# Gate weights written one loop step earlier, and the turning of keys and queries spread over two steps, in an attention and expert kernel

## The chip, the cores and the metric

The kernel runs as one program on 1 core of a Trainium2 chip. The metric is the device time of one execution in microseconds (us), lower is better. The kernel before took 427.58 us (median of 3 runs, 426.6 to 427.71).

## The reference

Two computations follow each other. First, attention in chunks: 4 batches of 8 heads, 768 tokens, 64 channels. A chunk of 32 queries sees 8 memory keys and at most 56 keys around the chunk.

```python
for c in range(nc):                                   # 24 chunks of 32 queries
    k_full = np.concatenate([mem_k, k_ctx], axis=2)
    v_full = np.concatenate([mem_v, v_ctx], axis=2)
    scores = scale * np.matmul(q_c, k_full.transpose(0, 1, 3, 2))
    scores = scores - np.max(scores, axis=-1, keepdims=True)
    a = np.exp(scores)
    a = a / (np.sum(a, axis=-1, keepdims=True) + 1e-09)
    out[:, :, c_start:c_end] = np.matmul(a, v_full)
```

Its result, 3072 tokens of 512 channels, goes through a layer of 8 experts. Each token goes to the one expert with the largest logit:

```python
logits = x @ w_gate + modality_bias[modality_id]
e_idx = np.argmax(logits, axis=1)
for e in range(E):
    mask = e_idx == e
    h = np.maximum(x[mask] @ w1[e], 0.0)
    out[mask] = gate_w[mask, None] * (h @ w2[e])
```

## The kernel before, in words

The 32 heads are taken in 16 pairs, u = 0 to 15. The main loop has two steps for each pair, i = 2u for the first half of its queries (hf 0) and i = 2u + 1 for the second (hf 1), and two more at the end, 34 in all. The text counts steps and pairs from 0, as the code does, so "the ninth step" is step 8, and the sixth pair is pair 5. All five instruction streams run in the order in which the program is written; nothing reorders them.

The work is a pipeline. In step i TensorE (PE) computes the scores of half i (`scores`, L328), turns the exponents' input of half i - 1 (`trans_p`, L345), turns keys or queries of the next pair, turns the attention output of half i - 2 (`trans_x`, L382) and multiplies half i - 1 with the values (`attend`, L357). VectorE (DVE) subtracts the row maximum (`less_max`, L336 and L339) and divides by the row sum (`normalize`, L365 to L370). ScalarE (ACT) takes the exponent (L347) and copies what PE has turned from PSUM to SBUF.

The part that the change touches prepares pair u + 1 while pair u is computed. Before it, step 2u turned the keys of both heads (`trans_k`, L310 and L314), which ACT copied into the block-diagonal key tile `kbd` in four copies (`store_k`, L320); DVE regrouped the queries (`regroup_q`, L277) into the single buffer `qr`. Step 2u + 1 then turned both halves of the queries (`trans_q`, L292), which ACT copied to `qT` (`store_q`, L297). `kbd` has two buffers, a pair's own being u % 2. What PE turns goes through four PSUM banks taken in rotation (`bank`).

GpSimd (POOL) copies the rows that neighbouring chunks share within the value tile `vw` (`share`, L267), writes the memory keys (`mem_keys`, L302), and issues the stores of the attention output to DRAM (`store_x`, L375). SyncE (SP) issues all loads of q, k and v in order: at the end of step 2u the values of pair u + 2 (`load_v`, L254 to L256), the memory values (`load_mv`, L263) and the keys and queries of pair u + 4 (`load_qk`, L93).

After each four pairs (one batch) the routing of its tokens starts, a generator `route(b)` of which `pump` issues a few instructions at a time between those of the steps. Its first matmuls (L530) read the gate weights `wg3`, which `gate_weights` (L233 to L235) writes on POOL; the bias rows come from `bias_rows` behind it. Their small loads are issued in step 5 (L170 to L173). Later the routing builds one-hot tables on POOL (the first two tiles) and DVE (the others), L656 and L659, which PE multiplies (L667) before it goes on. After the loop come the experts, up to L1300, with weights that SP loads by the routing's result.

```python
        if i == 9:
            gate_weights()
            bias_rows()
```

Of the kernel before, what the change touches and what calls it, by code (L numbers as in the profile page):

```python
# [37 lines left out]
NPOOL = 2  # L38
NSPIN = 8
NVW = 3  # L40
ORDERED = {mybir.EngineType.PE, mybir.EngineType.SP, mybir.EngineType.Pool, mybir.EngineType.Activation, mybir.EngineType.DVE}


@with_exitstack
def tile_chunk_attention_top1_moe(
# [14 lines left out]
    nc = tc.nc  # L60
    scale = 1.0 / float(D) ** 0.5
    NU = B * H // 2

    ctx.enter_context(tc.manual_schedule(engines=ORDERED))
    const = ctx.enter_context(tc.tile_pool(name="const", bufs=1))
# [17 lines left out]
    def bank():  # L83
        return ps.tile([P, 512], F32, name="tr", tag="tr", bufs=4)

    q2s, k2s = {}, {}
# [25 lines left out]
    kbds = [(pers if i else rt).tile([P, NCH, 2, 64], F32, name=f"kbd{i}") for i in range(2)]  # L112
    vws = [(rt if i == 1 else pers).tile([P, 2, NCH, D + 1], F32, name=f"vw{i}") for i in range(NVW)]
    zero = const.tile([P, 1], F32, name="zero")
# [14 lines left out]
    def blank_v(i, parts=1):  # L129
        for h in range(2):  # L130
            for k in range(parts):
                c = slice(NCH * k // parts, NCH * (k + 1) // parts)
                nc.gpsimd.memset(vws[i][64 * (1 - h):64 * (2 - h), h, c].rearrange("p c d -> p (c d)"), 0.0)
# [99 lines left out]
    def gate_weights():  # L233
        nc.gpsimd.memset(wg3, 0.0)
        nc.gpsimd.tensor_copy(wg3.rearrange("p c (q x) -> p c q x", x=40)[:, :, :, 0:E], wg.unsqueeze(2).to_broadcast([P, 4, 3, E]))  # L235
# [9 lines left out]
    qrs, qTs, xTs, xbs, PTs, kts, qts, scs, sbs, avs = ({} for _ in range(10))  # L245

    def load_v(u):
        vw = vws[u % NVW]
        for h in range(2):
            hh = 2 * u + h  # L250
            r0 = 64 * h

            src = bass.AP(tensor=vf.tensor, offset=(hh * S + 8) * D, ap=[[D, 32], [32 * D, NCH - 1], [1, D]])
            nc.sync.dma_start(vw[r0 + 24:r0 + 56, h, 0:NCH - 1, 0:D], src)  # L254
            nc.sync.dma_start(vw[r0 + 24:r0 + 48, h, NCH - 1, 0:D], vf[hh * S + S - 24:hh * S + S])
            nc.sync.dma_start(vw[r0 + 16:r0 + 24, h, 0, 0:D], vf[hh * S:hh * S + 8])  # L256

    def load_mv(u):
        vw = vws[u % NVW]
        for h in range(2):  # L260
            hh = 2 * u + h
            r0 = 64 * h
            nc.sync.dma_start(vw[r0 + 56:r0 + 64, h].rearrange("p c d -> p (c d)"), mvx[hh // 16][8 * (hh % 16):8 * (hh % 16) + 8].rearrange("p c d -> p (c d)"))  # L263

    def share(u, h, copy):
        vw, r0 = vws[u % NVW], 64 * h
        copy(vw[r0:r0 + 24, h, 1:NCH, 0:D], vw[r0 + 32:r0 + 56, h, 0:NCH - 1, 0:D])  # L267

    def share_v(u):
        for h in range(2):  # L270
            share(u, h, nc.gpsimd.tensor_copy)

    def regroup_q(u):
        q2 = q2s.pop(u)
        qr = qrs[u] = wk.tile([P, 6, 2, D], F32, name="qr", bufs=1)
        eng = nc.gpsimd if u in (1, 2) else nc.vector
        eng.tensor_copy(  # L277
            qr.rearrange("p x h d -> p h x d"), q2.rearrange("p (h a) (j d) -> p h (a j) d", h=2, j=2)
        )

    def warm(t, k):
        for _ in range(k):
            nc.tensor.matmul(t, idle[:, 0:P], idle[:, P:640], start=True, stop=True)

    def trans_q(u):
        qr = qrs.pop(u)
        for j in range(2):
            t = qts[u, j] = bank()
            if u == 1 and j == 0:
                warm(t, 5)  # L290
            for i in range(3):
                nc.tensor.transpose(t[:, i:3 * P:3], qr[:, 2 * i + j].rearrange("p h d -> p (h d)"), ident)  # L292

    def store_q(u, j):
        if j == 0:
            qTs[u] = wk.tile([P, S], F32, name="qT")
        nc.scalar.copy(qTs[u].rearrange("p (s j) -> p s j", j=2)[:, :, j], qts.pop((u, j))[:, 0:384])  # L297

    def mem_keys(u, eng):
        for h in range(2):  # L300
            r = slice(64 * h, 64 * h + 64)
            eng.tensor_copy(kbds[u % 2][r, :, h, 56:64], memT[r, u:u + 1, :].to_broadcast([64, NCH, NMEM]))  # L302

    def trans_k(u):
        k2 = k2s.pop(u)
        for h in (1, 0):
            hh = 2 * u + h
            t = kts[u, h] = bank()
            for i in range(3):
                nc.tensor.transpose(t[:, 9 + i:9 + i + 3 * P:3], k2[:, 3 * h + i, :], ident)  # L310

            pads = bass.AP(tensor=t.tensor, offset=t.offset + 1, ap=[list(t.ap[0]), [392, 2], [1, 8]])
            mem_sel = ident[:, 4 * hh:4 * hh + 4].unsqueeze(1).unsqueeze(1)
            nc.tensor.matmul(pads, mkp, mem_sel.to_broadcast([P, 2, 2, 4]), start=True, stop=True)  # L314

    def store_k(u, h, j, copy):
        tt = kts[u, h][64 * j:64 * j + 64]
        win = bass.AP(tensor=tt.tensor, offset=tt.offset + 1, ap=[list(tt.ap[0]), [16, NCH], [1, 28]])
        dst = kbds[u % 2][64 * h:64 * h + 64, :, h, 0:56]
        copy(dst.rearrange("p c (i j) -> p c i j", j=2)[:, :, :, j], win)  # L320
# [30 lines left out]
    def attend(u, hf):  # L351
        vw, PT = vws[u % NVW], PTs.pop((u, hf))
        avb = avs[u, hf] = ps.tile([P, 512], F32, name="av", tag="av", bufs=2)
        for t in range(3):
            for j in range(4):
                c = 4 * (3 * hf + t) + j
                nc.tensor.matmul(  # L357
                    avb[32 * j:32 * j + 32, t * W:(t + 1) * W], PT[:, t * P + 32 * j:t * P + 32 * j + 32],
                    vw[:, :, c, :], start=True, stop=True,
                )  # L360
# [32 lines left out]
    def pump(k, pe=(), late=False):  # L393
        if now[0] >= 2 * NU - 6 and not late:
            return
        while k > 0 and routing:
            g, wait, b, since = routing[0]
            if wait:
                if wait not in pe or since == now[0] and b < B - 2:
                    return  # L400
                pe = ()
            r = next(g, None)
            if r is None:
                routing.pop(0)
                return
            routing[0] = (g, r if r != "v" else None, b, now[0])
            k -= r == "v"
# [524 lines left out]
    def first_keys(u, copy):  # L932
        for h in range(2):
            r = slice(64 * h, 64 * h + 64)
            copy(kbds[u][r, :, h, 56:64], memp[r, u * NMEM:(u + 1) * NMEM].unsqueeze(1).to_broadcast([64, NCH, NMEM]))

    first_keys(0, nc.vector.tensor_copy)
    trans_q(0)
    store_q(0, 0)
    store_q(0, 1)  # L940
# [13 lines left out]
    n = len(units)  # L954
    for i in range(n + 2):
        live = i < n
        u, hf = units[i] if live else (NU, i % 2)
# [9 lines left out]
        if live:  # L967
# [11 lines left out]
                nc.vector.tensor_copy(memT.rearrange("p u m -> p (u m)"), memp[:, 0:P])  # L979
                load_mv(2)  # L980
            pump(1)
        if u + 1 < NU and hf == 0:
            if 0 < u < NU - 2:
                mem_keys(u + 1, nc.gpsimd)
            trans_k(u + 1)
            if 0 < u < NU - 2:
                regroup_q(u + 1)
            if u == 1:
                blank_v(2)
            pump(1)  # L990
            store_k(u + 1, 1, 0, nc.scalar.copy)
            if u == 0:
                first_keys(1, nc.scalar.copy)
            store_k(u + 1, 1, 1, nc.scalar.copy if u > 3 else nc.vector.tensor_copy)
            if u > 0:
                store_k(u + 1, 0, 0, nc.scalar.copy)
            store_k(u + 1, 0, 1, nc.scalar.copy if u > 0 else nc.vector.tensor_copy)
            pump(1)
        elif u + 1 < NU:
            if u == 0:  # L1000
                store_k(1, 0, 0, nc.scalar.copy)
            if u == NU - 2:
                share(u + 1, 0, nc.gpsimd.tensor_copy)
            else:
                share_v(u + 1)
            trans_q(u + 1)
            store_q(u + 1, 0)
            store_q(u + 1, 1)
            pump(3)
        elif live:  # L1010
            pump(3)
# [42 lines left out]
                routing.append((route(u2 // 4), "tiled", u2 // 4, i))  # L1054
        for _ in range(4 if i > 2 and hf == 1 else 0):
            next(constants, None)
        if i == 9:
            gate_weights()
            bias_rows()
        if i == 5:  # L1060
            nc.scalar.copy(mvx[1][:, :, 0:D], mvn[:, 1:2].to_broadcast([P, NCH, D]))
        if i == n - 5:
            regroup_q(NU - 1)
        if i < n:
            pump(1, ("tiled",))
        if i < 2:
# [1 line left out]
        if live and hf == 0 and u >= 1:  # L1068
            if u - 1 + NVW < NU:
                load_v(u - 1 + NVW)  # L1070
# [256 lines left out]
```

## Time and profile before

| | us |
|---|---|
| median of 3 runs | 427.58 |
| the profiled execution's own time | 428.59 |
| its span, first to last instruction | 426.8 |
| PE busy | 407.6 (95%) |
| DVE busy | 334.1 (78%) |
| ACT busy | 298.6 (70%) |
| POOL busy | 238.6 (56%) |

The span is the time from the first to the last instruction of the profiled execution; its own time is longer by what lies around the span. Busy times are sums over instructions of an engine. A wait is idle time of an engine ahead of an instruction, put down to what released it.

### The profile page before, as it was taken

The page shows a single profiled execution, that of the slowest core. Times are in us where ns is not written, and L with a number is a line of the kernel's source. Part 1 is how long each engine was busy: PE and PEld are TensorE (multiplying, and loading weights), DVE is VectorE, ACT ScalarE, POOL GpSimd, SP SyncE. Part 2 cuts the span into 40 slices and gives each one's busy share as a digit, 9 for nine tenths or more (in the row PEclk, how much of TensorE's full clock was granted, in tenths as well). Part 3 has the DMA queues.
Part 4 walks back from the last instruction along what each step waited for, and adds up shares of the span by engine and source line. Part 5 has one row for each costly group of instructions (what it writes and reads, how often), then busy time and mean ns, then how long its engine had stood idle before and what let it go on. Part 6 is the DMA issues. An engine that isn't in the chain of part 4 may idle for free.

```text
span 426.8 us, 11396 instructions
## 1 busy us (share of the span) xinstructions
PE 407.6 (95%) x3872; PEld 342.6 (80%) x3875; DVE 334.1 (78%) x788; ACT 298.6 (70%) x594; POOL 238.6 (56%) x320
## 2 busy tenths in 40 slices
PE   8899699999899999999999999999999999999993
PEld 5678478888776888989898887888888788888882
DVE  6989468879687878958979889768789787988750
ACT  7677667868685556746657677868878676888750
POOL 8886567668583445767754574354666266520101
PEclk9999999999999999999999999999999999999998
DMA  9899899999957920125423729979776514320101
GB/s 221 146 261 228 193 235 210 223 239 192 232 156 201 271 52 1 55 77 121 99 78 72 272 64 266 290 231 297 231 282 196 157 54 102 73 77 2 50 3 55
DMA packets 82543, 66.81 MB, mean 157 GB/s; under 512 B 50659, under 2 KB 71339, under 8 KB 82476
## 3 DMA queue, kind: packets, MB, share of 16 engines
q1 hardware_dynamic: 75276, 46.36, 45.0%
q0 software_dynamic: 6784, 19.50, 15.0%
q8 instruction: 33, 0.54, 0.5%
q14 instruction: 34, 0.28, 0.2%
q10 hardware_dynamic: 416, 0.13, 0.1%
HBM read 84.64 MB, written 12.76 MB: 228 GB/s over the span
## 4 chain that ended last, share of the span: by engine, by line
PE 71%; issue 12%; ACT 6%; POOL 4%; DVE 4%; DMA 2%; POOLq 0%; ACTq 0%
PE av L842 12%; PE tr L830 11%; PE sc L842 10%; PE tr L811 9%; PE av L357 5%; PE tr L814 5%; ACT kbd L320 4%; PE sc L328 4%; PE tr L382 3%; PE tr L345 2%; PE tr L292 2%; PE tr L310 2%; PE tr L530 2%; DMA out_dram<-o,ix_now 1%; POOL xg L751 1%
## 5 line engine op out<-in xcount | busy, mean ns | idle before, releaser
L811 PE MATMUL tr<-xt,w 128*128 128x512 f32 x256 | 70.1, 395 | 0.0
L742 DVE TENSOR_TENSOR w<-raw,w 128x512 fp32r<-128x512 f32 x96 | 64.7, 719 | 4.0 <-ACT w L741 3.2
L842 PE MATMUL av<-wh,h 128*128 128x512 f32 x192 | 61.5, 393 | 0.0
L267 POOL COPY vw<-vw 24x1472 f32<-24x1472 f32 x31 | 44.2, 1425 | 21.8 <-DMA vw<-in_v_dram 20.6
L741 ACT CAST w<-raw 128x512 fp32r<-128x512 f32 x96 | 53.9, 623 | 1.5 <-DMA raw<-in_moe_w_dram 1.5
L842 PE MATMUL sc<-wh,h 128*128 128x512 f32 x160 | 50.8, 392 | 0.0
L811 PEld LDWEIGHTS tr<-xt,w 128*128 128x128 f32 x256 | 44.3, 189 | 7.2 <-issue 0.8
L830 PE MATMUL tr<-xt,w 128*128 128x256 f32 x384 | 48.1, 284 | 0.7 <-DVE xt L806 0.7
L830 PEld LDWEIGHTS tr<-xt,w 128*128 128x128 f32 x384 | 46.8, 191 | 2.0 <-DVE xt L806 1.0
L320 ACT COPY kbd<-tr 64x672 f32<-64x672 f32 x57 | 44.5, 781 | 4.3 <-DVE kbd L320 2.3
L814 PEld LDWEIGHTS tr<-xt,w 128*128 128x128 f32 x256 | 39.2, 189 | 5.4
L847 POOL DMA_INDIRECT out_dram<-o,ix_now x22 | 26.1, 1184 | 29.6 <-ACT o L846 24.3
L842 PEld LDWEIGHTS av<-wh,h 128*128 128x128 f32 x192 | 36.0, 188 | 7.5 <-issue 0.2
L814 PE MATMUL tr<-xt,w 128*128 128x256 f32 x256 | 40.7, 281 | 0.0
L820 DVE TENSOR_TENSOR hs<-tr,hs 128x256 f32<-128x256 f32 x64 | 26.8, 419 | 17.6 <-ACT hs L817 17.6
L842 PE MATMUL av<-wl,h 128*128 128x512 f32 x96 | 37.5, 390 | 0.0
L821 ACT ACTIVATE h<-hs 128x256 fp32r<-128x256 f32 x64 | 26.8, 419 | 14.8 <-DVE hs L820 13.7
L751 POOL DMA_INDIRECT xg<-gd,gx x24 | 27.1, 1128 | 14.7 <-DMA gd<-gt 9.0
L842 PEld LDWEIGHTS sc<-wh,h 128*128 128x128 f32 x160 | 30.0, 188 | 6.3 <-issue 0.2
L823 DVE TENSOR_TENSOR wl<-vw,wh 128x512 fp32r<-128x512 f32 x48 | 33.2, 691 | 2.2
L824 DVE SCALAR_TENSOR_TENSOR h<-hs,h 128x256 fp32r<-128x256 f32 x64 | 27.7, 433 | 7.7 <-ACT h L821 7.3
L776 POOL COPY planes<-xg 128x1024 uint16<-128x1024 uint16 x18 | 24.0, 1339 | 17.0 <-DMA xg<-xd,gx 16.9
(266 smaller groups left out, 910.4 us busy)
## 6 DMA issues: line engine op xcount, KB each, us to landing
raw<-in_moe_w_dram SPq DMA_DIRECT2D x96, 256.0 KB
vw<-in_moe_w_dram SPq DMA_DIRECT2D x72, 256.0 KB
k<-in_k_dram SPq DMA_DIRECT2D x16, 384.0 KB
q<-in_q_dram SPq DMA_DIRECT2D x16, 384.0 KB
xd<-xb POOLq DMA_DIRECT2D x16, 384.0 KB
kbd<-in_moe_w_dram SPq DMA_DIRECT2D x24, 256.0 KB
vw<-in_v_dram SPq DMA_DIRECT2D x32, 184.0 KB
xall<-in_moe_w_dram SPq DMA_DIRECT2D x4, 1024.0 KB
```

The costliest lines, as they stand in the source:

```text
L267: copy(vw[r0:r0 + 24, h, 1:NCH, 0:D], vw[r0 + 32:r0 + 56, h, 0:NCH - 1, 0:D])
L320: copy(dst.rearrange("p c (i j) -> p c i j", j=2)[:, :, :, j], win)
L741: nc.scalar.copy(wh[i], raw[i])
L742: (eng or nc.vector).tensor_sub(wl[i], raw[i], wh[i].bitcast(F32))
L751: nc.gpsimd.indirect_dma_start(out=xg[t][:, part], out_offset=None, in_=rows, in_offset=bass.IndirectOffsetOnAxis(ap=gx[:, t:t + 1], axis=0))
L811: nc.tensor.matmul(ph, wh[f][:, c * P:(c + 1) * P], xt[:, c].rearrange("p a n -> p (a n)"), start=(c == 0), stop=False, skip_group_check=True)
L814: nc.tensor.matmul(ph[:, 0:256], wl[f][:, c * P:(c + 1) * P], xth[:, c], start=False, stop=(c == 3), skip_group_check=True)
L820: nc.vector.tensor_add(hs, ph[:, 0:256], hs)
L823: nc.vector.tensor_sub(wl[w], raw[w], wh[w].bitcast(F32))
L824: nc.vector.scalar_tensor_tensor(hl[:, f], hs, 0.0, hh[:, f].bitcast(F32), op0=ALU.max, op1=ALU.subtract)
L830: nc.tensor.matmul(ph, w[f][:, c * P:(c + 1) * P], x[:, c, :], start=(n == 0), stop=(n == 11))
L842: nc.tensor.matmul(pos[t], x, w[8 + f], start=(f == 0 and n == 0), stop=(f == 7 and n == 2))
```

## The change

`gate_weights` and `bias_rows` are issued in step 8 and not in step 9. From pair 5 on (`AHEAD`), a step with hf 0 turns the keys of head 1 and the first half of the queries of the next pair, and a step with hf 1 turns the second half of these queries and then the keys of head 0 of the pair after the next, which it also regroups the queries of. The copies that ACT makes of them move with them. The last pair's `regroup_q`, which stood at the end of step 27, falls under the same rule.

```diff
+AHEAD = 5
...
-    def trans_q(u):
-        qr = qrs.pop(u)
-        for j in range(2):
+    def trans_q(u, js=(0, 1)):
+        qr = qrs[u]
+        for j in js:
             t = qts[u, j] = bank()
...
-    def trans_k(u):
-        k2 = k2s.pop(u)
-        for h in (1, 0):
+    def trans_k(u, hs=(1, 0)):
+        k2 = k2s[u]
+        for h in hs:
...
-        if u + 1 < NU and hf == 0:
+        if AHEAD <= u < NU - 1 and hf == 0:
+            if u < NU - 2:
+                mem_keys(u + 1, nc.gpsimd)
+            trans_k(u + 1, (1,))
+            pump(1)
+            store_k(u + 1, 1, 0, nc.scalar.copy)
+            store_k(u + 1, 1, 1, nc.scalar.copy)
+            trans_q(u + 1, (0,))
+            store_q(u + 1, 0)
+            pump(1)
+        elif u + 1 < NU and hf == 0:
             if 0 < u < NU - 2:
                 mem_keys(u + 1, nc.gpsimd)
             trans_k(u + 1)
-            if 0 < u < NU - 2:
+            if 0 < u < AHEAD:
                 regroup_q(u + 1)
...
-            trans_q(u + 1)
-            store_q(u + 1, 0)
+            if u < AHEAD:
+                trans_q(u + 1)
+                store_q(u + 1, 0)
+            else:
+                trans_q(u + 1, (1,))
             store_q(u + 1, 1)
+            if AHEAD <= u + 1 < NU - 1:
+                trans_k(u + 2, (0,))
+                store_k(u + 2, 0, 0, nc.scalar.copy)
+                store_k(u + 2, 0, 1, nc.scalar.copy)
+                regroup_q(u + 2)
             pump(3)
...
-        if i == 9:
+        if i == 8:
             gate_weights()
             bias_rows()
...
-        if i == n - 5:
-            regroup_q(NU - 1)
```

On POOL, around steps 8 and 9, the kernel before has this order. The copies of `vw_114` are the shared rows of pair 5, `kbd_111` and `kbd_110` take the memory keys of pairs 5 and 6, and L234 to L242 are the gate weights and the bias rows:

```order
L302 COPY kbd_111<-memT 64x24x8 x2
L267 COPY vw_114<-vw_114 24x23x64 x2
L375 DMA xd<-xb 128x6x128
L234 MEMSET wg_135 128x480
L235 COPY wg_135<-wg 128x12x8
L238 MEMSET mods 25x128
L239 CAST mods<-mod_i 24x128
L240 TENSOR_TENSOR bias_b<-bias_b 24x8
L242 TENSOR_TENSOR rows_b<-bias_b,ident 24x192
L302 COPY kbd_110<-memT 64x24x8 x2
```

The changed kernel has there:

```order
L303 COPY kbd_111<-memT 64x24x8 x2
L235 MEMSET wg_135 128x480
L236 COPY wg_135<-wg 128x12x8
L239 MEMSET mods 25x128
L240 CAST mods<-mod_i 24x128
L241 TENSOR_TENSOR bias_b<-bias_b 24x8
L243 TENSOR_TENSOR rows_b<-bias_b,ident 24x192
L268 COPY vw_114<-vw_114 24x23x64 x2
L376 DMA xd<-xb 128x6x128
L303 COPY kbd_110<-memT 64x24x8 x2
```

The six instructions moved past the two copies of `vw` and past the issue of one store, and nothing else on POOL moved.

On PE, steps 10 and 11 of the kernel before read as follows, from the scores of step 10 on (`k_587` holds the keys of pair 6):

```order
L328 MATMUL sc<-kbd_111,qT 32x128 x12
L345 MATMUL tr<-ident,sb 128x128 x3
L310 MATMUL tr<-ident,k_587 128x128 x3
L314 MATMUL tr<-ident,mkp 128x2x8
L310 MATMUL tr<-ident,k_587 128x128 x3
L314 MATMUL tr<-ident,mkp 128x2x8
L382 MATMUL tr<-ident,xb 128x128 x3
L357 MATMUL av<-vw_113,PT 32x130 x12
L530 MATMUL tr<-xall,wg_135 32x256 x12
L328 MATMUL sc<-kbd_111,qT 32x128 x12
L345 MATMUL tr<-ident,sb 128x128 x3
L292 MATMUL tr<-ident,qr 128x128 x6
```

In the changed kernel they are (`k_731` holds the keys of pair 7):

```order
L329 MATMUL sc<-kbd_111,qT 32x128 x12
L346 MATMUL tr<-ident,sb 128x128 x3
L311 MATMUL tr<-ident,k_587 128x128 x3
L315 MATMUL tr<-ident,mkp 128x2x8
L293 MATMUL tr<-ident,qr 128x128 x3
L383 MATMUL tr<-ident,xb 128x128 x3
L358 MATMUL av<-vw_113,PT 32x130 x12
L531 MATMUL tr<-xall,wg_135 32x256 x12
L329 MATMUL sc<-kbd_111,qT 32x128 x12
L346 MATMUL tr<-ident,sb 128x128 x3
L293 MATMUL tr<-ident,qr 128x128 x3
L311 MATMUL tr<-ident,k_731 128x128 x3
```

Half of the next pair's queries moved from step 11 into step 10, and in step 11 the keys of one head of pair 7 came in, which stood in step 12. Every second step up to step 27 has this form.

On DVE, from the maximum of step 10 to that of step 11, the kernel before has (`q_586` holds the queries of pair 6):

```order
L336 TENSOR_REDUCE mx<-sc 128x6
L339 TENSOR_TENSOR sb<-sc,mx 128x384
L277 COPY qr<-q_586 128x2x6x64
L365 TENSOR_SCALAR den<-av 128x6
L366 RECIPROCAL den<-den 128x6
L370 TENSOR_TENSOR xb<-av,den 128x384
L336 TENSOR_REDUCE mx<-sc 128x6
L339 TENSOR_TENSOR sb<-sc,mx 128x384
L545 TENSOR_REDUCE l<-tr 128x48
```

The changed kernel has (`q_730` holds the queries of pair 7):

```order
L337 TENSOR_REDUCE mx<-sc 128x6
L340 TENSOR_TENSOR sb<-sc,mx 128x384
L366 TENSOR_SCALAR den<-av 128x6
L367 RECIPROCAL den<-den 128x6
L371 TENSOR_TENSOR xb<-av,den 128x384
L337 TENSOR_REDUCE mx<-sc 128x6
L340 TENSOR_TENSOR sb<-sc,mx 128x384
L278 COPY qr<-q_730 128x2x6x64
L546 TENSOR_REDUCE l<-tr 128x48
```

The regrouping of each pair's queries stands one step earlier, from pair 6 on, and the number of instructions on DVE is the same.

## Rows read from the trace of the kernel before

**Rows 1.** The page, part 1: busy us, share of the span, instructions.

```profile
PE 407.6 (95%) x3872; PEld 342.6 (80%) x3875; DVE 334.1 (78%) x788; ACT 298.6 (70%) x594; POOL 238.6 (56%) x320
```

**Rows 2.** Timeline of PE: start, us, what ran, idle before it and releaser.

```profile
16.98 0.86 PE L328 MATMUL sc<-kbd,qT 128*32 128x128 f32 x24 [1.11 <-ACT qT L297]
...
47.49 0.87 PE L357 MATMUL av<-vw,PT 128*32 128x130 f32 x24
51.44 2.78 PE L530 MATMUL tr<-xall,wg 128*32 128x256 f32 x24 [3.08 <-POOL wg L235]
...
55.21 0.55 PE L345 MATMUL tr<-ident,sb 128*128 128x128 f32 x3
...
81.87 0.87 PE L357 MATMUL av<-vw,PT 128*32 128x130 f32 x24
...
84.63 0.55 PE L345 MATMUL tr<-ident,sb 128*128 128x128 f32 x3
```

**Rows 3.** Windows: length, busy PE, PEld, DVE, ACT, POOL; PEclk, DMA share, GB/s.

```profile
16.98:20.43 3.45, 3.44 (x64) 3.01 (x68) 3.29 (x8) 2.02 (x3) 2.50 (x5) 1.00 0.91 124
51.44:54.90 3.46, 3.46 (x44) 2.15 (x48) 0.00 (x0) 0.37 (x1) 2.49 (x7) 0.51 1.11 247
55.88:61.24 5.36, 5.36 (x104) 4.77 (x106) 3.88 (x15) 3.50 (x8) 2.60 (x5) 1.00 1.06 237
100.24:107.82 7.58, 7.58 (x133) 6.34 (x133) 7.20 (x22) 6.26 (x13) 6.07 (x9) 1.00 1.02 179
109.05:115.10 6.05, 6.02 (x119) 5.28 (x122) 3.91 (x13) 2.21 (x5) 3.05 (x5) 1.00 1.14 263
```

**Rows 4.** Timeline of POOL, steps 8 to 10.

```profile
41.69 0.74 POOL L302 COPY kbd<-memT 64x192 f32<-64x192 f32 x2
46.64 3.10 POOL L267 COPY vw<-vw 24x1472 f32<-24x1472 f32 x2 [4.22 <-DMA vw<-in_v_dram]
...
50.56 0.50 POOL L234 MEMSET wg<- 128x480 f32 x1
...
52.59 0.73 POOL L302 COPY kbd<-memT 64x192 f32<-64x192 f32 x2
```

**Rows 5.** Waits of PE from 60 to 200 us: total, times, longest.

```profile
PE tr L292 <- ACT kbd L320: 2.2, 6, 0.7
```

**Rows 6.** Waits of SP from 48 to 116 us: total, times, longest.

```profile
SPq L263 <- DMA q<-in_q_dram: 11.8, 9, 1.9
...
SPq L263 <- DMA k<-in_k_dram: 1.4, 4, 0.4
```

**Rows 7.** Timeline of SP's issues.

```profile
39.33 0.90 SPq L170 DMA_DIRECT2D wg<-in_moe_w_gate_dram  x1
...
55.88 0.40 SPq L254 DMA_DIRECT2D vw<-in_v_dram  x1
...
100.24 0.40 SPq L254 DMA_DIRECT2D vw<-in_v_dram  x1
...
104.43 2.89 SPq L263 DMA_DIRECT2D vw<-mvx  x2
...
109.05 0.35 SPq L254 DMA_DIRECT2D vw<-in_v_dram  x1
```

**Rows 8.** Timeline of PE in steps 25 and 29.

```profile
106.67 1.05 PE L292 MATMUL tr<-ident,qr 128*128 128x128 f32 x6
...
126.10 0.91 PE L667 MATMUL tr<-a,l 128*128 128x192 f32 x6
```

**Rows 9.** Timeline of POOL, shared rows of pairs 7, 13, 14 and one-hot tables.

```profile
61.24 1.62 POOL L267 COPY vw<-vw 24x1472 f32<-24x1472 f32 x1 [2.65 <-DMA vw<-in_v_dram]
...
107.82 1.41 POOL L267 COPY vw<-vw 24x1472 f32<-24x1472 f32 x1 [1.28 <-DMA vw<-in_v_dram]
...
116.57 2.88 POOL L267 COPY vw<-vw 24x1472 f32<-24x1472 f32 x2
...
124.45 1.00 POOL L659 TENSOR_SCALAR a<-iota,ac,tokm 128x192 fp32r<-128x192 f32 x1
```

## The prediction

> **What bounds the kernel now.** I read the busy times of the engines first, then the waits of PE, then PE's timeline around each wait, then the timelines of POOL and SP for what stands behind these waits, and last the windows for the clock and the load of the DMA engines. PE is busy for 407.6 of 426.8 us [rows 1], so this is a kernel that goes as fast as PE's stream does, and an edit gains only where it takes an idle stretch out of that stream. There are two kinds that the edits reach. One is large: PE stands for 3.08 us before the first routing matmuls, L530, until POOL has written the gate weights [rows 2]. The other is small and repeated: after 60 us the second turning of queries waits six times for ACT to empty a PSUM bank with its key copies, 2.2 us together, 0.7 at most [rows 5]. Beside both the reader is to see what does not hold PE up yet, SP's loads. The issue of the memory values, L263, is held nine times by the landing of a pair's queries and four times by that of its keys [rows 6], and the DMA engines show a share of 1.02 to 1.14 in three windows of the middle and the end [rows 3]. So loads come as fast as this queue brings them, and not when PE frees a buffer.
>
> **The gate weights.** POOL works in order. In steps 8 and 9 it finishes the memory keys at 41.69 + 0.74 = 42.43, then stands 4.22 us for the values of pair 5, copies them from 46.64 on, and only then writes the gate weights from 50.56 on [rows 4]. In the new order the six instructions fall into that idle stretch. They take 52.59 - 50.56 = 2.03 us [rows 4], so they are done at about 44.5, before 46.64, and the copies behind them start when they did. The copy from `wg` needs its load, issued at 39.33 [rows 7]; the trace does not show its landing. The slowest load that I measured below takes 7.58 us, which would be 46.9, and PE's L530 is due at about 48.2 (below), so at either end PE does not wait. In the slow case the copies of pair 5 start 1 to 2 us late, and they are not used before step 11.
>
> What the wait costs is more than its 3.08 us. From the start of the multiplication with the values to the turning of the next step PE needs 55.21 - 47.49 = 7.72 us here, and 84.63 - 81.87 = 2.76 us in the same sequence eight steps later [rows 2]. The difference is 4.96 us. The rest of it, 1.88 us, is the clock: the granted clock is 0.51, so 1.2 of 2.4 GHz, in the 3.46 us after the wait [rows 3]. I take 4.96, with L530 at 47.49 + 0.7 = 48.2.
>
> **The turning of keys and queries.** It adds no instruction on any engine; PE, ACT and DVE do the same work a step earlier or later. On ACT a step had four key copies and the next had none; now each has two and one query copy, so the bank that the second query turning wanted is emptied sooner, and I take all 2.2 us [rows 5]. What speaks for it is that the wait names ACT's key copy and nothing else. The moved regrouping on DVE waits for `qr`, its only buffer, until PE has turned the second half of the queries in the same step; behind it on DVE stands `normalize`, which PE's next `trans_x` needs. That cover was there before, since DVE stood idle ahead of `normalize` in most steps.
>
> Both together: 4.96 + 2.2 = 7.16 us, if nothing else comes late. The sum is made against the profiled execution, 428.59 us (a span of 426.8 with 1.79 around it), which lies 1.01 above the median of 427.58. Everything gained would put the median at 420.4.
>
> **What is late next.** All these loads stay where they are in time, and PE would arrive 5 to 7 us earlier, and it needs the keys one step earlier too. Two places decide.
>
> In step 25 the keys of pair 14, head 0, are now turned in the middle of what was the query turning, 106.67 + 0.5 = 107.2 in the old clock [rows 8]. These keys are there only when SP's L263 at 104.43 gets through [rows 7]. So at this point PE can be at most 107.2 - 104.4 = 2.8 us ahead, whatever it had gained; of the six small waits those of steps 27 and 29 can still be added after it, at most 2 x 0.7 = 1.4.
>
> In step 29 PE multiplies the one-hot tables of the third batch, L667, at 126.10 [rows 8]. POOL's part of the tables is ready at 124.45 + 1.00 = 125.45, and it is at the end of a chain on POOL that begins with the shared rows of pair 14 at 116.57 and is 125.45 - 116.57 = 8.88 us long [rows 9]. That chain cannot begin before the values of pair 14 have landed. Their load is issued at 109.05 [rows 7]; the trace doesn't show its landing, since in the kernel before POOL was late for it. Two loads that POOL did wait for took 61.24 - 55.88 = 5.36 us and 107.82 - 100.24 = 7.58 us [rows 7, 9], the first while the DMA engines moved 237 GB/s, the second at 179. The stretch from 109.05 on moved 263 [rows 3], so I stay near the first and take 6.0: landed at 115.05, tables at 123.93, PE at about 124.0, which is 2.1 us before 126.10. With 5.36 the gain is 2.7; with 7.58 the chain begins no earlier than now and only the 0.65 between 125.45 and 126.10 are left, about 0.55.
>
> So of 7.16 us about 2.1 pass step 29. Behind it the experts' phase starts from this point, and its first loads and tables hang on the same POOL chain, so I let the 2.1 reach the end: 428.59 - 2.1 = 426.5 for a profiled run, 425.5 for the median.
>
> **The clock in the new waits.** In this forecast PE stands about 2.8 + 1.0 - 2.1 = 1.7 us before L667. A wait of 1.11 us left the granted clock at 1.00 in the stretch behind it, the wait of 3.08 us was followed by 0.51 [rows 2, 3]; 1.7 lies nearer the first, so I charge nothing. [...]
>
> **The rivals.**
> 1. POOL's tables are not late (the values land sooner, or PE is later), and only the keys of step 25 bind: 2.8 to 4.2 us, I take 3.5, median 424.1. For it: the stretch is the fastest of the three. Chance 0.22.
> 2. The loads move up as PE does, and the whole 7.16 is kept: 420.4. For it: buffers come free earlier. Against it: L263 waits for landings and not for buffers [rows 6]. The Trainium skill, page DMA: Bandwidth & Descriptors, section Specifications, gives about 358 GB/s from memory to one core; by it the loads have room at 263 and the sum would be this one. The trace speaks against it with its DMA share above 1 at 179 to 263 GB/s. Chance 0.07.
> 3. The wait before L667 halves the clock and costs a further 1.88 us: 0.2 is left, 427.4. Chance 0.10.
> 4. Slower: POOL reaches output stores earlier than before, these go in front of the values of pair 14, and the load takes longer than both that I measured: the slower one plus their difference once more, 7.58 + 2.22 = 9.8 us. The values land at 118.85, the tables are ready at 127.73, and PE is at 127.8, 1.7 us later than before: 430.3 for a profiled run, 429.3 for the median. It decides from a landing after 117.2 on (116.57 + 0.65) and shows as slower from 118.5. Against it: each store stands on POOL behind copies that themselves wait for values. Chance 0.05.
> 5. The change doesn't do what it says: the gate weights' load lands after 48, and part of the wait at L530 stays. The 2.2 us and the bounds above leave 0 to 2, I take 1.0, 426.6. Chance 0.03.
>
> **How the numbers follow.** The forecast has 0.53, with its own range of 424.9 to 427.0 (2.7 and 0.55). About 0.3%, 1.28 us, is what a measurement of this kernel can tell from no change. The forecast is beyond it unless the values take more than 6.8 us; I give four fifths of it, 0.42, to faster and 0.11 to no change. With rivals 1 and 2 and a third of the fifth, faster is 0.72; no change is 0.11 + 0.10 + 0.02 = 0.23; slower 0.05. From 423.0 to 427.4 holds the forecast, the third and fifth rival and nearly all of the first, and leaves out the second, the fourth and a rest of the first, some 0.15.
>
> **What would show it.** The wait at L530 is gone, and the granted clock is 1.00 throughout steps 9 to 12; POOL writes the gate weights (now L235 and L236) at about 42.5 to 43.5. No wait of L292 (now L293) on ACT after step 10. In their place stand new waits of PE on keys just landed (L311) between steps 13 and 25, and one of 1 to 2 us before the L668 of step 29 put down to POOL's tables; DVE waits for queries ahead of L278. SP issues the values of pair 14 at 109 plus or minus 1. The forecast is wrong if SP's issues after 60 us come several us earlier than before, or if PE passes step 29 more than 3 us early or later than before.

## The result and the profile after

The changed kernel took 422.94 us (median of 12 runs) against 426.58 of before, run beside it; the ratio is 0.9916 with a 95% interval of 0.9891 to 0.9940, so 3.6 us faster (2.6 to 4.6). A second comparison gave 0.9893 (0.9854 to 0.9932), 4.6 us. The forecast was 2.1 us of gain, 425.5, with 423.0 as its low end. The direction was right and the gain about 1.7 times as large. The time of 422.94 lies just below that low end, and 1.0 us of its distance to the forecast is the baseline's: the three runs that the forecast started from had a median of 427.58, these twelve 426.58. Counted as a gain, 3.6 us is inside the 4.6 that the low end allowed; what the forecast had wrong is how the time comes about.

The profiled execution took 421.46 us, its span 419.7, against 428.59 and 426.8 before. That pair differs by 7.1 us, more than the medians do. Some 1.8 of it stands in steps 0 to 7, ahead of every changed instruction: step 8 begins at 36.12, before at 37.90. The medians decide on size, and the traces on place.

The wait for the gate weights is gone. PE's timeline in steps 10 and 11 after [rows 2], then POOL's in steps 9 and 10 [rows 4] (start, duration, engine, line, operation; in brackets the idle time before it and who ended it). Lines behind the new constant are one higher than before.

```profile
45.86 0.87 PE L358 MATMUL av<-vw,PT 128*32 128x130 f32 x24
46.55 1.48 PE L531 MATMUL tr<-xall,wg 128*32 128x256 f32 x24
47.84 0.84 PE L329 MATMUL sc<-kbd,qT 128*32 128x128 f32 x24
48.61 0.55 PE L346 MATMUL tr<-ident,sb 128*128 128x128 f32 x3
```

```profile
40.29 0.50 POOL L235 MEMSET wg<- 128x480 f32 x1
41.44 0.26 POOL L236 COPY wg<-wg 128x96 f32<-128x96 f32 x1 [0.64 <-DMA wg<-in_moe_w_gate_dram]
...
42.82 0.51 POOL L243 TENSOR_TENSOR rows_b<-bias_b,ident 24x192 f32<-24x192 f32 x1
44.30 2.88 POOL L268 COPY vw<-vw 24x1472 f32<-24x1472 f32 x2 [0.98 <-DMA vw<-in_v_dram]
```

The six instructions lie in POOL's idle stretch; the copy waits 0.64 us for its load and still ends nearly 5 us before L531. From the values' multiplication to the turning of step 11 PE needs 48.61 - 45.86 = 2.75 us, where before it needed 7.72. The granted clock is full where it was 0.51 [rows 3]; the windows row of after (window, its length, busy time of each engine, clock, DMA share, GB/s):

```profile
46.50:50.00 3.50, 3.50 (x71) 2.78 (x62) 2.35 (x6) 2.51 (x6) 2.19 (x4) 1.00 1.05 290
```

PE's waits over the whole span after (engine, line, releaser: us in total, times, longest). The query turning's wait on ACT [rows 5] has shrunk to one of 0.2, and new ones stand in its place, on the keys and, 2.9 us where the trace of before has 1.0, on DVE's `xb`:

```profile
PE tr L383 <- DVE xb L371: 2.9, 7, 0.5
...
PE tr L311 <- DMA k<-in_k_dram: 1.1, 1, 1.1
...
PE tr L531 <- ACT xall L386: 0.6, 1, 0.6
PE tr L311 <- issue: 0.5, 1, 0.5
...
PE tr L293 <- ACT kbd L321: 0.2, 1, 0.2
```

What the forecast did not have is in SP's timeline [rows 7]. The values of pair 13 are issued at 95.62 (before 100.24), those of pair 14 at 103.87 (before 109.05):

```profile
95.62 0.40 SPq L255 DMA_DIRECT2D vw<-in_v_dram  x1
...
103.87 0.84 SPq L255 DMA_DIRECT2D vw<-in_v_dram  x1
```

The waits of SP on landed queries, between 40 and 128 us, are smaller than in [rows 6]. That is not the change's doing: the second traces of the two kernels, from runs further below, have 8.6 us before and 8.7 after.

```profile
SPq L264 <- DMA q<-in_q_dram: 7.2, 7, 1.6
...
SPq L264 <- DMA k<-in_k_dram: 1.0, 2, 0.5
```

### The profile page after: what moved, and what is told of

It reads as the page before. It is cut to its first block, busy times and chain, and to the rows that moved or that the text cites. A ratio compares the mean times of both kernels' runs of the same rounds, so it can differ in the third digit from the quotient of the medians.

```text
span 419.7 us, 11402 instructions
## 1 busy us (share of the span) xinstructions
PE 402.2 (96%) x3875; PEld 340.6 (81%) x3875; DVE 338.8 (81%) x788; ACT 301.4 (72%) x594; POOL 238.8 (57%) x320
## 4 chain that ended last, share of the span: by engine, by line
PE 63%; issue 13%; DMA 10%; POOL 6%; DVE 5%; ACT 1%; POOLq 1%; SPq 0%; ACTq 0%; DVEq 0%
PE av L843 12%; PE tr L831 11%; PE sc L843 10%; PE tr L812 9%; PE tr L815 5%; PE av L358 3%; DMA vw<-in_v_dram 3%; DMA q<-in_q_dram 2%; PE sc L329 2%; DMA k<-in_k_dram 2%; DMA out_dram<-o,ix_now 1%; PE tr L383 1%; PE tr L346 1%; PE tr L311 1%; POOL vw L268 1%
## 5 line engine op out<-in xcount | busy, mean ns | idle before, releaser
L743 DVE TENSOR_TENSOR w<-raw,w 128x512 fp32r<-128x512 f32 x96 | 68.0, 752 | 3.9 <-ACT w L742 3.6
L812 PE MATMUL tr<-xt,w 128*128 128x512 f32 x256 | 70.1, 395 | 0.0
L821 DVE TENSOR_TENSOR hs<-tr,hs 128x256 f32<-128x256 f32 x64 | 26.8, 419 | 13.3 <-ACT hs L818 13.2
L752 POOL DMA_INDIRECT xg<-xd,gx x24 | 27.8, 1157 | 8.7 <-issue 4.8
```

The source lines that it names most:

```text
L743: (eng or nc.vector).tensor_sub(wl[i], raw[i], wh[i].bitcast(F32))
L752: nc.gpsimd.indirect_dma_start(out=xg[t][:, part], out_offset=None, in_=rows, in_offset=bass.IndirectOffsetOnAxis(ap=gx[:, t:t + 1], axis=0))
L812: nc.tensor.matmul(ph, wh[f][:, c * P:(c + 1) * P], xt[:, c].rearrange("p a n -> p (a n)"), start=(c == 0), stop=False, skip_group_check=True)
L821: nc.vector.tensor_add(hs, ph[:, 0:256], hs)
```

## The experiments

Theory A is the forecast's: the loads stay where they are in time, and the one-hot tables of step 29 bind. B: the loads move up with PE, and nothing later binds. P: PE, once early, runs into the loads and gives part back. Q: the missing part was never there, because the long wait stands in some executions only. F: the loads run at a pace of their own, different in each execution.

This table is worked out from the timelines of PE and SP: where the first scores of step 11 start, and how long step 10, steps 16 to 18 and steps 11 to 29 take, from first scores to first scores; and SP's first issue for the values of pair 13.

| kernel | step 11 at | step 10 | steps 16-18 | steps 11-29 | values 13 |
|---|---|---|---|---|---|
| before | 53.98 | 9.10 | 11.74 | 72.96 | 100.24 |
| before again | 53.58 | 9.10 | 11.76 | 72.16 | 98.68 |
| before, dummies in the wait | 51.32 | 8.07 | 11.77 | 72.63 | 95.72 |
| gate weights alone | 48.23 | 4.59 | 13.11 | 74.39 | 97.00 |
| turning alone | 50.20 | 6.88 | 11.52 | 70.20 | 96.65 |
| changed | 47.84 | 4.39 | 14.35 | 72.09 | 95.62 |
| changed again | 49.49 | 4.39 | 13.31 | 72.00 | 95.94 |
| changed, 20 dummies | 55.22 | 8.95 | 11.57 | 68.89 | 100.90 |
| changed, fewer loads | 49.35 | 4.38 | 12.06 | 70.15 | 91.97 |
| changed, keys first | 50.14 | 4.39 | 13.29 | 71.22 | 97.15 |

### The gate weights alone

```diff
 (in the kernel before)
-        if i == 9:
+        if i == 8:
             gate_weights()
             bias_rows()
```

> The kernel before with the gate weights and bias rows written one step earlier on GpSimd, and the old turning of keys and queries. Theory A (the forecast: loads stay where they are in time, step 29's one-hot tables bind): the wait before the routing matmuls goes (3.1 us and the clock's 1.9), but POOL's tables of step 29 hold PE again, gain 1 to 2.5 us in the median. Theory B (the loads move up with PE, nothing later binds): 3 to 5 us of gain, clock 1.00 in steps 9 to 12, SP's issues after 60 us earlier by as much. The six waits of the query turning on ACT's key copies (2.2 us) stay in either.

Ratio 0.9955 (0.9918 to 0.9992): 1.9 us faster. By its size this is what theory A gave, but not by its place: L667 in step 29 has no wait on POOL, and its loads are issued 3.2 us earlier than in the trace of before, 2.0 if both are counted from the start of step 8, which lies ahead of the change. Step 10 is 4.5 us shorter; then steps 16 to 18 take 1.4 us more than in the three traces of the old turning that come to them later. Most of this is one stop in step 18 for which the trace has no releaser:

```profile
76.92 0.44 PE L310 MATMUL tr<-ident,k 128*128 128x128 f32 x2 [1.15 <-issue]
```

From step 8 to step 30 the trace is 2.3 and 3.1 us shorter than the two traces of before, so part of the 4.5 us is given back on the way.

### The turning alone

```diff
 (in the changed kernel)
-        if i == 8:
+        if i == 9:
             gate_weights()
             bias_rows()
```

> The changed kernel with the gate weights back in the tenth step: only the turning of one head's keys and half the queries is new. Theory A: the 2.2 us of bank waits go and nothing else binds at so small a lead, gain about 2 us; the wait of about 3 us before the routing matmuls stays, with a clock of 0.51 behind it. Theory B (the turning only trades waits on ACT for waits on xb, keys and queries): 0 to 0.6 us.

Ratio 0.9948 (0.9915 to 0.9980): 2.2 us faster (0.9 to 3.6), beside the 2.2 us of the forecast's term. The two halves alone add up to 4.1 us, in agreement with 3.6 and 4.6 for both. The wait for the gate weights was 2.27 us in this trace, and behind it the granted clock stayed full. The profiled run, 421.82 us, is one of the faster ones: 7 of the 12 runs had a mean granted clock below 0.995 over the whole run and a median of 425.05 us, the other 5 had 422.4.

```profile
48.88 1.50 PE L531 MATMUL tr<-xall,wg 128*32 128x256 f32 x24 [2.27 <-POOL wg L236]
```

```profile
49.20:52.70 3.50, 3.50 (x64) 2.82 (x56) 1.56 (x3) 1.46 (x4) 2.42 (x6) 1.00 1.06 219
```

### The kernel before and the changed kernel once more

> The kernel before once more, for a second trace of it. Theory F (the loads run at a pace of their own, which differs from one execution to the next, and the trace on which the forecast rests had a late one): SP issues the first values of pair 13 at 95 to 98 and not at 100.2, although PE again comes to step 11 at 51 to 54, and the wait for the gate weights is anywhere from 2.3 to 4.3 us. Theory B (the loads follow PE): the values of pair 13 are issued 46 us behind the start of step 11, as in the trace of before.

> The changed kernel once more, beside the others on the same chip. About 3.6 us faster than before again (3 to 5). Theory A would now need POOL's tables to be late in step 29 of some run; theory B says no wait there again, and SP's issues of the memory values at a mean distance near 7.0 us, or, if the pace of the loads varies from run to run and not with PE, anywhere from 6.9 to 7.4.

Before took 426.84 us in its one run. Its wait was again 3.07 us and the clock behind it 0.55:

```profile
51.04 2.78 PE L530 MATMUL tr<-xall,wg 128*32 128x256 f32 x24 [3.07 <-POOL wg L235]
```

```profile
51.40:54.90 3.50, 3.50 (x49) 2.15 (x42) 0.00 (x0) 0.37 (x1) 2.78 (x6) 0.55 1.12 259
```

The values of pair 13 came at 98.68, which is 45.1 us behind the start of step 11, where theory B said 46 and theory F 95 to 98. It falls between them and decides nothing. The changed kernel again took 4.6 us less than before, with no wait at L668, and again with long steps 16 to 18 (13.31 us) and a wait on the keys of pair 10 (0.44 us). Its issues of memory values lie 7.11 us apart in the mean (pairs 6 to 15), against 7.03 in the first trace and 7.53 and 7.32 in the two of before, which fits either of the two accounts.

### Dummy work in the wait of the kernel before

```diff
         lg = bank()
+        warm(lg, 10 if b == 0 else 0)
```

> The kernel before with ten dummy matmuls of 512 columns on PE ahead of the first routing matmuls (2.2 us of work in the place of the wait for the gate weights; the result isn't touched). The wait itself stays, only the idle time shrinks to under 1 us. If the clock's share of the wait is as in before's trace, 1.88 us, in every run, the median falls by about 1.9 us. If the low clock stands only in the runs with a mean clock below 0.995 (about 6 in 10 of before's), it falls by about 1.1 us, and no run with a mean clock below 0.995 is left. If the clock has no part in it: 0, or 0.5 slower.

Ratio 0.9982 (0.9953 to 1.0010): 0.8 us faster, and that may be nothing. No run of the 12 had a mean clock below 0.995, so the dummies did keep the clock up; the wait itself stayed (2.33 us of dummies and 1.00 idle):

```profile
46.66 2.33 PE L283 MATMUL tr<-idle 128*128 128x512 bf16 x10
50.00 1.50 PE L531 MATMUL tr<-xall,wg 128*32 128x256 f32 x24 [1.00 <-POOL wg L235]
```

Of the 63 runs of before that three of the comparisons count, 42 had a mean clock below 0.995 and a median of 426.8 us, 21 had more and 424.6. That the expensive form of the wait stands in two of three executions is an estimate from these counts. Both traces of before have the long wait, and none shows this kernel without it; the mean clock is no sure sign either, since 3 of 20 runs of the changed kernel, which has no such wait in either of its traces, lie below 0.995 too. The 2.1 us between the two groups are more than the dummies brought back. A possible reason is that with the dummies the wait was still 3.3 us long, against 2.27 in the trace of the turning alone, where the clock had stayed up by itself.

### Twenty dummies in the changed kernel

```diff
         lg = bank()
+        warm(lg, 20 if b == 0 else 0)
```

> The changed kernel with twenty dummy matmuls of 512 columns ahead of the first routing matmuls (4.5 us of work on PE, result untouched), so that PE comes to step 11 about as late as before and the turning stays new. Theory F: the values of pair 13 are still issued at 95 to 98, PE no longer waits for the keys of pair 10 in step 17, steps 16 to 18 take 11.5 to 12 us together instead of 13 to 14.4, and the time is only 2 to 3 us above the changed kernel's. Theory B: the loads shift by 4.5 us too, and so does the time.

Ratio against before 0.9985 (0.9951 to 1.0019), so about 3 to 4 us above the changed kernel, for 4.5 us of work. In the traces step 11 comes 7.38 us later than in the changed kernel, but 2.82 of that stands ahead of step 10, in the start, and the loads were as late there (pair 6 by 2.85). Behind it PE loses 4.56 us and the values of pair 13 lose 2.43. Their issue at 100.90 does not settle theory F, since without the late start it would stand at about 98, the edge of F's range.

Pair 14 tells more, the pair that step 29 hangs on. Counted from the start of step 8, its values are issued after 70.1 to 71.2 us in the three traces with a late step 11 (before, before again, twenty dummies), and after 67.8 to 68.8 in the three with an early one (changed, changed again, gate weights alone); step 11 itself differs by 4.1 to 4.7 us between them. So the loads do move with PE, by about half, and theory F alone does not hold. Over the first eight rows of the table, with everything counted from step 8, a line through step 11 and the values has a slope of 0.48 for pair 13 and 0.53 for pair 14.

The steps behind are short when PE is late, as theory P has it and theory F had expected too: PE does not wait for keys, steps 16 to 18 take 11.57 us, and of the 4.56 us only 1.36 are left at step 30. By the runs less comes back, some 1 of 4.5 us, so the size of this stays open.

### Fewer loads, in both kernels

```diff
-                load_mv(u - 1 + NVW)
+                if u - 1 + NVW < 6:
+                    load_mv(u - 1 + NVW)
```

> The changed kernel without the two loads of memory values per pair from pair 6 on (the memory rows of an earlier pair stay in the buffer, so this part of the result is left out): SP issues two loads of 1.07 us less per pair, and the waits on landed queries and keys ahead of them go too. Theory P (PE, once ahead, runs into the loads and gives back part of the 4.96 + 2.2 us there): 1.5 to 3 us faster than the changed kernel, the waits on k gone. Theory Q (the loads follow PE and hold nothing up; the missing part was never there, because the long wait and its slow clock stand in some runs of before only): within 0.7 us of the changed kernel.

> The kernel before without the same loads of memory values from pair 6 on (left out of the result). Both theories: no wait of PE on a load was in before's trace, so the time stays within 0.7 us of before; with theory P the difference between this kernel and the changed one without these loads grows to 5 us or more, with theory Q it stays at 3 to 4.5 us. If the time falls by more than 1 us, before was held by SP's loads in a way that the list of PE's waits doesn't show (POOL's copies of the values of pair 5 and behind it the gate weights come sooner).

The whole times, 462.29 and 468.30 us, cannot be set beside the other runs: other memory values route other tokens to the experts, and the phase behind the loop became some 40 us longer, which I had not thought of. Between the two of them they can: this phase takes 341.0 and 341.2 us in their traces, and the difference of 6.0 us is what theory P asked for (5 or more) and not theory Q (3 to 4.5). Part of it may be the wait for the gate weights, 4.28 us in this trace of the kernel before. Up to step 30 the traces can be compared with the others. With fewer loads the changed kernel has no wait on keys from step 6 to the end of the loop, only those on DVE and ACT:

```profile
PE tr L383 <- DVE xb L371: 3.1, 6, 0.7
PE tr L293 <- DVE kbd L321: 0.7, 1, 0.7
PE tr L531 <- ACT xall L386: 0.7, 1, 0.7
```

Its steps 16 to 18 take 12.06 us and its steps 11 to 29 70.15, against 72.09 and 72.00. In the kernel before, fewer loads leave both as they were (11.77 and 73.43). That is theory P: loads cost the changed kernel nearly 2 us there, and the kernel before nothing. The waits on `xb` are as large as with all loads, so they are not the loads'. Only part of the 2 us is a named wait in the changed kernel: 1.10 us on keys and a stop of 0.51 without a releaser, 0.44 and 0.77 in its second trace.

### The order of loads

```diff
 (in the changed kernel, at the end of step 2u)
-                load_mv(u - 1 + NVW)
             if u + 4 < NU:
                 load_qk(u + 4)
+            if u - 1 + NVW < NU:
+                load_mv(u - 1 + NVW)
```

> The changed kernel with each pair's keys and queries issued by SP ahead of the two loads of memory values instead of behind them (2.13 us of issuing and the waits for landed queries ahead of the keys go). If being early is given back to late keys and queries in steps 16 to 18 (1.4 to 2.8 us against the kernel with the old gate weights), this is 1 to 2 us faster than the changed kernel and the keys of pair 10 land 2 us earlier, at 69 to 70. If the DMA engines and not SP's order set the landing: 0. If the memory values come late in their place: slower, with waits of PE or POOL on vw.

Ratio 0.9889 (0.9851 to 0.9927), beside 0.9893 and 0.9916 for the changed kernel: no difference that these runs can tell. The wait on keys is gone and one on values has come, 2.5 us over two times, 1.57 of it in step 7 and 0.89 in step 17; PE also waits 0.61 us in step 16 for POOL's tables:

```profile
PE av L358 <- DMA vw<-in_v_dram: 2.5, 2, 1.6
```

So here the order chose which of the loads is late.

The other way to take the memory values out of SP's row is to let POOL issue them, from pair 6 on:

```diff
 (in the changed kernel)
-            nc.sync.dma_start(vw[r0 + 56:r0 + 64, h].rearrange("p c d -> p (c d)"), mvx[hh // 16][8 * (hh % 16):8 * (hh % 16) + 8].rearrange("p c d -> p (c d)"))
+            (nc.gpsimd if u >= 6 else nc.sync).dma_start(vw[r0 + 56:r0 + 64, h].rearrange("p c d -> p (c d)"), mvx[hh // 16][8 * (hh % 16):8 * (hh % 16) + 8].rearrange("p c d -> p (c d)"))
```

> The changed kernel with the memory values of pairs 6 and up loaded from GpSimd's queue instead of SP's (same bytes, nothing left out). Theory P, if SP's order and not the bytes hold the loads: 1 to 2 us faster than the changed kernel. If the bytes do it: 0. If POOL, which stands for landed values up to 2.5 us at a time, issues them late: 0 to 2 us slower, with waits of PE on vw.

Ratio 0.9952 (0.9920 to 0.9985), 2.0 us faster than before, so some 2 us slower than the changed kernel. The memory values come in time, but PE waits for POOL's tables in step 29, in the place where the forecast had seen the bound. The last table is ready 0.47 us later than in the changed kernel's trace (119.52), with two more issues for each pair on POOL, and PE comes to step 29 0.94 us earlier:

```profile
118.04 0.36 PE L668 MATMUL tr<-a,l 128*128 128x192 f32 x1
119.58 0.80 PE L668 MATMUL tr<-a,l 128*128 128x192 f32 x5 [1.18 <-POOL a L660]
```

### The regrouping of queries behind the normalization

```diff
-                regroup_q(u + 2)
                 pump(3)
 ...
             normalize(*units[i - 1])
             pump(1)
+        if live and hf == 1 and AHEAD <= u + 1 < NU - 1:
+            regroup_q(u + 2)
```

> The changed kernel with the regrouping of the next but one pair's queries on VectorE put behind the normalization instead of ahead of it. If the seven new waits of PE on xb (2.9 us together in the changed kernel's trace) come from the regrouping that stands on DVE ahead of the normalization, they go back to about 1 us and the time falls by 1 to 2 us against the changed kernel. If they are queries landing late or PE merely being early, the time stays within 0.5 us and the waits reappear under another name.

Ratio 1.0155 (1.0095 to 1.0216): 6.6 us slower than before, some 11 slower than the changed kernel. Neither expectation held. The waits on `xb` did fall to 0.5 us, but PE, which turns these queries at the start of the next step, now waits for them:

```profile
PE tr L293 <- DVE qr L278: 9.0, 7, 2.5
PE tr L293 <- DVE me L558: 3.6, 2, 2.9
```

The routing's table work, which `pump` puts behind the normalization, stands ahead of the regrouping on DVE (its timeline in step 16 of this kernel):

```profile
67.97 0.47 DVE L660 TENSOR_SCALAR a<-iota,ac,tokm 128x192 fp32r<-128x192 f32 x1
68.36 0.34 DVE L657 TENSOR_SCALAR l<-iota,lo 128x130 fp32r<-128x130 f32 x1
68.61 0.46 DVE L660 TENSOR_SCALAR a<-iota,ac,tokm 128x192 fp32r<-128x192 f32 x1
68.99 1.72 DVE L278 COPY qr<-q 128x768 f32<-128x768 f32 x1
```

So the changed kernel's place ahead of the normalization, at up to 0.5 us of wait on `xb` a time (1.0 once in its second trace), is the cheap one of the two.

## Why the prediction was wrong, step by step

**The gate weights: right in place.** The instructions went into POOL's idle stretch, the wait is gone, the clock is full, and 4.96 us of gross gain became 4.7 in step 10 (9.10 to 4.39). As a price for every execution it was probably too high: where the wait is 2.27 us and the clock stays up, as in the trace of the turning alone, step 10 has only 6.88 - 4.39 = 2.5 to give.

**The turning: right in direction, and in size partly by luck.** 2.2 us forecast, 2.2 measured alone (0.9 to 3.6). The waits on ACT went, but 2.2 was their size in one trace (1.1 over the same stretch in the second), and waits on `xb` came in their place. PE's idle time in steps 11 to 29 is no smaller by it: 2.2 to 4.5 us in the five traces of the old turning, 1.5 to 5.0 in seven of the new. What fell is PE's busy time there: 69.5 to 70.5 us in the old, 67.4 to 68.1 in the new. So the listed waits were not what the turning gained: steps 20 and 21 are 7.16 us long before, with 0.35 listed as a wait, and 6.39 in the changed kernel, with none. What makes up the rest stays open.

**The step that failed is "All these loads stay where they are in time".** With it went the two bounds that I built on it, 2.8 us at step 25 and 2.1 us at step 29, and with the second the sum. The loads are issued 2.3 to 6.2 us earlier after than before, from pair 6 to pair 15 (the first values of each). About 2 of that is the earlier start, which moved step 8 by 1.78; counted from step 8 the loads follow PE by about half. For the values of pair 14 this is 3.4 us. With the forecast's own 6.0 us of landing, which no run shows, and 8.88 of chain, the bound at step 29 moves from 2.1 to 5.5 us, and PE comes there 5.2 us earlier, so nothing holds it. Both signs that the forecast named for being wrong are there: SP's issues after 60 us come 3.3 to 6.2 us earlier, and PE passes step 29 7.0 us earlier, 5.2 without the start. I had read the waits of one line of SP, L263 [rows 6], which are on landings, and concluded that buffers don't matter. The same view of the kernel before, for SP's other lines, has waits put down to PE and to engines that run in step with it, which empty buffers (40 to 128 us):

```profile
SPq L255 <- PE tr L382: 2.4, 4, 1.1
SPq L93 <- DVE mx L336: 2.2, 2, 1.1
...
SPq L254 <- POOL vw L267: 1.2, 3, 0.5
SPq L93 <- DVE sb L339: 1.1, 2, 0.8
SPq L255 <- PE tr L292: 1.0, 1, 1.0
```

These five come to 7.9 us, beside 17.4 on landings in the same stretch, 13.2 of it the queries and keys of rows 6. When PE and DVE go earlier, this part of the loads can go with them. That it is what moves the loads is read from these waits; no run tests it by itself.

**The chain of step 29 was not followed back far enough.** I let POOL's chain begin with the shared rows of pair 14 [rows 9] and took their landing as its earliest start. The row ahead of it was there to be read in the kernel before:

```profile
115.77 0.75 POOL L302 COPY kbd<-memT 64x192 f32<-64x192 f32 x2 [3.41 <-PE sc L328]
116.57 2.88 POOL L267 COPY vw<-vw 24x1472 f32<-24x1472 f32 x2
```

POOL stood 3.41 us for PE's scores of step 27, so this chain starts with PE and moves with it, as long as its values have landed. After, it is the same, 6.2 us earlier, and ends 0.04 us ahead of L668, so the place is a near miss; with the memory values on GpSimd's queue PE does wait there:

```profile
109.59 0.74 POOL L303 COPY kbd<-memT 64x192 f32<-64x192 f32 x2 [2.52 <-PE sc L329]
110.39 3.09 POOL L268 COPY vw<-vw 24x1472 f32<-24x1472 f32 x2
...
118.05 1.00 POOL L660 TENSOR_SCALAR a<-iota,ac,tokm 128x192 fp32r<-128x192 f32 x1
```

```profile
119.09 0.91 PE L668 MATMUL tr<-a,l 128*128 128x192 f32 x6
```

**Something is given back, but elsewhere.** The forecast let 5 of 7.16 us be lost to late loads; about 3 are missing, to these and, it seems, to executions whose wait was short. What is left at step 30 reaches the end, as the forecast had it: from there on the nine traces of the table with all loads take 299.3 to 301.3 us. The place of the loss is steps 16 to 18, where the changed kernel meets the loads of pairs 9 and 10. PE's timeline there:

```profile
66.73 0.68 PE L383 MATMUL tr<-ident,xb 128*128 128x128 f32 x3 [0.47 <-DVE xb L371]
...
71.76 0.52 PE L311 MATMUL tr<-ident,k 128*128 128x128 f32 x3 [1.10 <-DMA k<-in_k_dram]
...
75.45 0.27 PE L311 MATMUL tr<-ident,k 128*128 128x128 f32 x1 [0.51 <-issue]
```

The new wait on just landed keys between steps 13 and 25 was forecast; that it costs 1.1 us once and leaves the bound at step 25 slack was not. The two runs with fewer loads and with PE made late are what shows that these steps are long because PE comes early. Whether the stop in the last line is the loads' stays open.

**The rivals.** The first had the size, 3.5 us, and the half of its mechanism that the tables are not late because the values land sooner; its place, the keys of step 25, shows no wait, so the size is luck. The second (the loads move up and all 7.16 are kept) had the direction of the loads and the wrong size, since they follow by half only and it counted neither what PE gives back nor executions with a short wait; I held rows 6 and the DMA share against it and gave it 0.07. Of the rest, the third's clock loss before L667, the fourth's late values and the fifth's late gate weights did not come. The sum that the runs support is 1.9 for the gate weights and 2.2 for the turning. How the 1.9 comes about is an estimate: 4.7 in two of three executions and 2.5 in the others, less some 2 us given back.

**The clock.** 2.27 us of waiting left it at 1.00, so 2.4 GHz, and behind 3.07 and 3.08 us it was 0.55 and 0.51, near 1.2 GHz, as behind the 4.28 us in the kernel before with fewer loads (0.60). The Trainium skill, page TensorE: Matmul & The Clock Gate, section HAM oscillation, tells of a kernel that waits about 3 to 5 us for data between its bursts of matmuls and starts each next burst at the lower clock. The three waits from 3.07 us up agree with it; the one of 2.27 us is shorter than those it tells of.

## What to carry to other kernels

Before a load is taken as fixed in time, read every wait of the issuing queue, all its lines, and sort them into landings and buffers: the part that waits for buffers can move with the engine that is sped up. Of a chain that is to bind later, read one row further back, to what it waits for; if that is the engine being sped up, the chain moves along and binds only through its loads. And a long wait in one profiled execution is priced for the executions that have it: the mean clock of each run gives a first estimate of how many do.

## What the runs showed of the hardware that I had not expected

The regrouping copy on DVE (L278, 128x768) takes 0.56 us when POOL is idle and 1.59 us beside POOL's copy of the shared rows, in the changed kernel's timelines of DVE and POOL. From step 11 on its other two that begin beside such a copy take 1.71 and 1.33 us, all the rest 0.55 or 0.56:

```profile
73.32 0.56 DVE L278 COPY qr<-q 128x768 f32<-128x768 f32 x1 [1.63 <-DMA q<-in_q_dram]
80.44 1.59 DVE L278 COPY qr<-q 128x768 f32<-128x768 f32 x1
```

```profile
80.21 3.10 POOL L268 COPY vw<-vw 24x1472 f32<-24x1472 f32 x2 [1.50 <-DMA vw<-in_v_dram]
```

In step 18 PE stands between two transposes of one tile with no releaser in the trace, 0.51 us in the changed kernel, 0.77 in its second trace and 1.15 with the gate weights alone, but not with the turning alone or with fewer loads, which come to this step at much the same time. What it waits for stays open.
